# Block 3's layer-norm sums: ScalarE in place of VectorE, in a kernel with a state-space branch and a feed-forward branch

## The chip, the cores and the metric

The kernel runs on one core of a Trainium2 chip. The metric is the device time of one execution in microseconds (us). A profile gives the span from the first to the last instruction, which is about 1.8 us shorter than the time. The engines are named as in the profile: PE is TensorE, PEld its weight loads, DVE is VectorE, ACT is ScalarE, POOL is GpSimd, SP is the queue that issues the DMA transfers.

Executions of the kernel before lay between 177.4 and 178.6 us in all rounds of this study. All runs compared below are of the state that the records call fast.

## The reference, cut to what matters

```python
def reference(...):                      # x: 2048 rows of 512, bf16
    x = A_x
    xn = _layernorm(x, axis=-1)          # (x - mean) / sqrt(var + 1e-5)
    return x + _A_ref(xn, ...) + _B_ref(xn, ...)

# _A_ref: Bu = xn @ B_bar (complex, 512 states); h[t] = Lam_bar * h[t-1] + Bu[t]
#         y = 2 Re(h @ C) + xn * Dskip
# _B_ref: (gelu(xn @ w_gate) * (xn @ w_up)) @ w_down     # 512 -> 1376 -> 512
```

## The kernel before: the parts that the argument touches

The 2048 rows are four blocks of 512, each four tiles of 128 rows. A block goes through layer norm (VectorE), transposes (`TR`, by DMA), the input matmuls `BU` of the recurrence, `CHAIN` (VectorE: rotate, eight scans, rotate back), the hidden layer `GU` (two matmul groups per feature tile, evicted from PSUM by ScalarE, multiplied by VectorE), and the output matmuls `DN` (11 hidden tiles and 8 state tiles into one bank, added to the skip term by VectorE, stored). PSUM is the memory that the matmuls write, in banks; to evict is to copy a result out of a bank, so that the bank can be written again.

```python
def stats(b, j):
    tt = 4 * b + j
    return (V(lambda e: e.bn_stats(ST[tt].ap, X[tt].ap), ...),
            V(lambda e: e.bn_aggr(MVt[b][j].ap, ST[tt].ap), ...))

def LN(b, js=range(4)):
    for j in js:
        stats(b, j)                       # VectorE: 4 x statistics, 4 x aggregation
    _, mn, qb, rq = root(b, js[0], js[-1] + 1)   # VectorE + GpSimd: sqrt(var + eps)
    recip(qb, rq)                         # VectorE
    norms(b, js, mn, rq, js[0])           # VectorE: (x - mean) * rq, 4 tiles
...
    DN(0, True)
    LN(3); SKIP(3)
    GU(2, [0, 1, 2, 10, 3, 4, 5, 6, 7]); TR(3); GU(2, [8, 9])
    BU(3)
    CHAIN(3)
    DN(1, True)
    GU(3, [0, 1, 2, 10, 3, 4, 5, 6, 7, 8, 9])
    DN(2)
    DN(3, tail=384)
    S.schedule()
    S.emit()
```

TensorE and the DMA queue run in the order of the program text. For VectorE, ScalarE and GpSimd a list scheduler (`S.schedule`), with its own table of estimated durations, fixes the order when the kernel is built. So an edit in one place can reorder those three engines anywhere; TensorE's order stays.

Of the kernel before, what the change touches and what calls it, by code (L numbers as in the profile page):

```python
# [9 lines left out]
ALU = mybir.AluOpType  # L10
ACTF = mybir.ActivationFunctionType
BF16, F32, I32 = dt.bfloat16, dt.float32, dt.int32
# [330 lines left out]
L, D, P, F = 2048, 512, 512, 1376  # L343
# [5 lines left out]
EPS_BF16 = 1.0013580322265625e-05  # L349
# [3 lines left out]
def d_dve_tt2x(n): return 100.0 + 0.52 * n  # L353
def d_dve_1x(n): return 100.0 + 1.04 * n
def d_dve_scan(n): return 90.0 + 2.08 * n
def d_dve_ts4x(n): return 220.0 + 0.26 * n
D_TINY = 160.0
def d_act(n, ptr=0): return 190.0 + 0.833 * n + 90.0 * ptr
# [3 lines left out]
def build(nc, ins, out):  # L362
    with ExitStack() as es:
        E = es.enter_context
        S = Sched(nc, es)
        ARENA_BYTES = 207 * 1024
        arena_t = E(nc.sbuf_tensor("arena", [128, ARENA_BYTES // 2], BF16))
        A = Arena(arena_t, ARENA_BYTES)
# [3 lines left out]
        def ring(parent, name, n):  # L372
            return [A.sub(parent, "%s%d" % (name, i), i) for i in range(n)]
# [13 lines left out]
        X = ring(X_all, "X", NT)  # L387
        XN_all = A.alloc("XN", [8, D], BF16)
        XN = ring(XN_all, "XN", 8)
# [13 lines left out]
        SBQ = A.alloc("SBQ", [NB, 4], BF16)  # L403
        QB = A.alloc("QB", [NB, 4], BF16)
        RQ = A.alloc("RQ", [NB, 4], F32)
        HALF = A.alloc("HALF", [4], F32)

        def cols(buf, b, j0, j1):
            per = (buf.hi - buf.lo) // (4 * NB)
            return Buf("%s_%d_%d_%d" % (buf.name, b, j0, j1), "sb", buf.lo + per * (4 * b + j0), buf.lo + per * (4 * b + j1),  # L410
                       buf.ap[:, b, j0:j1])
# [48 lines left out]
        V = lambda fn, dur, r, w, tag="", after=(): S.op("vector", fn, dur, r, w, tag, after)  # L460
        ACT = lambda fn, dur, r, w, tag="", after=(): S.op("scalar", fn, dur, r, w, tag, after)
        POOL = lambda fn, dur, r, w, tag="", after=(): S.op("gpsimd", fn, dur, r, w, tag, after)
# [148 lines left out]
        def stats(b, j):  # L611
            tt = 4 * b + j
            return (V(lambda e: e.bn_stats(ST[tt].ap, X[tt].ap), d_dve_1x(512), [X[tt]], [ST[tt]], "bnst"),  # L613
                    V(lambda e: e.bn_aggr(MVt[b][j].ap, ST[tt].ap), D_TINY, [ST[tt]], [MVt[b][j]], "bnag"))

        def root(b, j0, j1):
            mn, sbq, qb, rq = (cols(t, b, j0, j1) for t in (MN, SBQ, QB, RQ))
            mv = Buf("MV%d_%d_%d" % (b, j0, j1), "sb", MVt[b][j0].lo, MVt[b][j1 - 1].hi, MV[b].ap[:, j0:j1])
            op = V(lambda e: e.tensor_scalar(sbq.ap, mv.ap[:, :, 1], EPS_BF16, None, ALU.add), D_TINY, [mv], [sbq], "sbq")
            GATE["pow"] = POOL(lambda e: e.tensor_tensor(qb.ap, sbq.ap, HALF.ap[:, 0:j1 - j0], ALU.pow), 1100, [sbq, HALF], [qb], "pow")  # L620
            POOL(lambda e: e.tensor_copy(mn.ap, mv.ap[:, :, 0]), 200, [mv], [mn], "mn")
            return op, mn, qb, rq

        def recip(qb, rq):
            return V(lambda e: e.reciprocal(rq.ap, qb.ap), 150, [qb], [rq], "rq")

        def norms(b, js, mn, rq, j0):
            last = None
            for j in js:
                tt, i = 4 * b + j, j - j0  # L630
                xs = XN[tt % 8]
                last = S.order_behind(V(lambda e, tt=tt, i=i, xs=xs: e.tensor_scalar(
                    xs.ap, X[tt].ap, mn.ap[:, i:i + 1], rq.ap[:, i:i + 1], ALU.subtract, ALU.mult),
                  d_dve_ts4x(512), [X[tt], mn, rq], [xs], "ln_n"), last)
            return last

        def LN(b, js=range(4)):
            for j in js:
                stats(b, j)
            _, mn, qb, rq = root(b, js[0], js[-1] + 1)  # L640
            recip(qb, rq)
            norms(b, js, mn, rq, js[0])

        def SKIP(b):
            for tt in range(4 * b, 4 * b + 4):
                xs = XN[tt % 8]
                V(lambda e, tt=tt, xs=xs: e.tensor_tensor(XD[tt].ap, xs.ap, DSKB.ap, ALU.mult),
                  d_dve_tt2x(512), [xs, DSKB], [XD[tt]], "skip")
# [59 lines left out]
        def TR(b):  # L708
            tts = list(range(4 * b, 4 * b + 4))
            for j, tt in enumerate(tts):  # L710
                S.dma(lambda e, b=b, j=j, tt=tt: e.dma_start_transpose(
                    XNT[b].ap[:, :, 128 * j:128 * (j + 1)], XN[tt % 8].ap),
                    1.6 * 128 * 1024, reads=[XN[tt % 8]], writes=[XTk[b][j]], tag="tr_x%d" % b, issue=1280.0)
# [264 lines left out]
        LN(1, [0, 1]); LN(1, [2, 3])  # L978
        TR(1)
        SKIP(0)  # L980
        GU(0, [7, 8, 9, 10])
        GATE["before_gelu"] = [tables_act([GATE["last_gelu"]])]
        SKIP(1)
        BU(0)
        CHAIN(0, 2)
        H0_T()
        BU(1)
        coefs()
        CHAIN(1)
        LN(2); SKIP(2)  # L990
        TR(2)
        load_C()
# [3 lines left out]
        BU(2)  # L996
        CHAIN(2)
        DN(0, True)
        LN(3); SKIP(3)
        GU(2, [0, 1, 2, 10, 3, 4, 5, 6, 7]); TR(3); GU(2, [8, 9])  # L1000
        BU(3)
        CHAIN(3)
# [9 lines left out]
def bass_parallel_sum__ssm_conv_s5__geglu_ffn__prompt_kernel(  # L1012
    nc: bass.Bass,
    A_x: bass.AP,
    A_Lambda_re: bass.AP,
    A_Lambda_im: bass.AP,
    A_B_re: bass.AP,
    A_B_im: bass.AP,
    A_C_re: bass.AP,
    A_C_im: bass.AP,  # L1020
    A_log_dt: bass.AP,
    A_Dskip: bass.AP,
    B_x: bass.AP,
    B_w_gate: bass.AP,
    B_w_up: bass.AP,
    B_w_down: bass.AP,
    out: bass.AP,
):
    ins = {
        "A_x": A_x, "A_Lambda_re": A_Lambda_re, "A_Lambda_im": A_Lambda_im,  # L1030
        "A_B_re": A_B_re, "A_B_im": A_B_im, "A_C_re": A_C_re, "A_C_im": A_C_im,
        "A_log_dt": A_log_dt, "A_Dskip": A_Dskip,
        "B_w_gate": B_w_gate, "B_w_up": B_w_up, "B_w_down": B_w_down,
    }
    build(nc, ins, out)
# [28 lines left out]
```

## Time and profile before

| | before |
|---|---|
| time, median | 177.95 us (3 runs before the prediction), 177.81 us (6 runs with the change's rounds) |
| span | 176.2 us |
| busy: PE / DVE / ACT / POOL | 173.6 / 162.3 / 90.3 / 9.8 us |
| matmuls | 891 |

The first lines of the page give the busy time of each engine, its share of the span, and its number of instructions:

```profile
PE 173.6 (99%) x891; PEld 84.9 (48%) x891; DVE 162.3 (92%) x283; ACT 90.3 (51%) x169; POOL 9.8 (6%) x25
```

Two engines are nearly full, and a busy share cannot tell which of them sets the pace. The chain of waits can. It follows the work that ended last back to the start; each line is start, duration, and what ran. This is its end:

```profile
87.48 12.09 PE PS L812 x56
99.57 6.91 PE PS L723 x32
106.47 16.42 PE PS L853 x76
...
141.48 32.91 PE PS L853 x171
174.38 0.02 issue
174.41 0.29 DVE arena L871
```

Each piece starts where the one before it ends, and 16.42 us / 76 = 216 ns per matmul in every long piece of 512 columns (the last piece, x171, also has narrower matmuls). The Trainium skill ("TensorE: Matmul & The Clock Gate", section "Wait — 56ns, not 53.3ns?") gives 215.7 ns start to start for back-to-back matmuls of 512 columns with the clock fully granted, so these stretches have no gap to win.

Where the change acts, by the windows view. The columns after the stretch are its length, then the busy time (and instructions) of PE, PEld, DVE, ACT, POOL, the granted TensorE clock, the DMA share and GB/s:

```profile
70.00:82.00 12.00, 12.00 (x57) 5.48 (x56) 10.12 (x26) 0.38 (x2) 1.29 (x2) 1.00 0.10 33
82.00:142.00 60.00, 60.00 (x300) 28.62 (x298) 58.96 (x74) 32.61 (x62) 0.00 (x0) 1.00 0.10 25
```

The reader should see 0.38 of 12 us for ScalarE in the first stretch, and 58.96 of 60 for VectorE in the second: VectorE is nearly as full as TensorE there. ScalarE's timeline says that its idle time lasts 11.6 us, until the first GELU eviction of block 2 (the brackets give the idle time before an instruction, and what ended it):

```profile
69.25 1.06 ACT L727 ACTIVATE arena<-PS 128x512 bf16<-128x512 f32 x2
81.94 0.60 ACT L827 ACTIVATE arena<-PS 128x512 bf16<-128x512 f32 x1 [11.62 <-PE PS L812]
```

VectorE's timeline: the statistics of block 3, its last normalisations, and, much later, the last piece of block 3's recurrence, which the last output matmuls need:

```profile
72.63 1.87 DVE L613 BATCH_NORM_STATS2 arena<-arena 128x6 f32<-128x512 bf16 x3
...
81.96 0.73 DVE L632 TENSOR_SCALAR arena<-arena 128x512 bf16<-128x512 bf16 x2
...
162.69 1.22 DVE L772 TENSOR_TENSOR arena<-arena 128x2048 bf16<-128x2048 bf16 x1
```

That last piece ends at 163.91 us. The matmuls that read it come after 109 others of the stretch that starts at 141.48 us (76 of block 2 and 33 of block 3's hidden part): 141.48 + 109 x 0.216 = 165.0 us. So VectorE is 1.1 us ahead of TensorE at the end.

### The profile page before, as it was taken

To read this page: it belongs to the slowest core of one execution; us is meant where nothing else is said; L and a number is where in the kernel's file an instruction comes from. 1 tells how busy PE (TensorE), PEld (TensorE's weight loads), DVE (VectorE), ACT (ScalarE), POOL (GpSimd) and SP (SyncE) were. 2 spreads that over 40 slices of the span, in tenths; PEclk is the share of its full clock that TensorE was granted. 3 is DMA by queue.
4 is the path that set the end of the run, shared out by engine and by line. 5 is a ranking of instruction groups with operands and counts; after the bars stand their busy time and mean duration, and the time that the engine had idled before them with its cause. 6 is when DMAs were issued, how large, how long until landed. Compare 5 with 4: busy or idle time off the path is not lost.

```text
span 176.2 us, 2504 instructions
## 1 busy us (share of the span) xinstructions
PE 173.6 (99%) x891; PEld 84.9 (48%) x891; DVE 162.3 (92%) x283; ACT 90.3 (51%) x169; POOL 9.8 (6%) x25
## 2 busy tenths in 40 slices
PE   8999999999999999999999999999999999999995
PEld 3854464444644444444644444444464444444454
DVE  6788999986999999979999999989999999999981
ACT  5566558899876899002676793000667790000000
POOL 3222030210000000011000000000000000000000
PEclk9999999999999999999999999999999999999999
DMA  5996997984998000012015000002101000000141
GB/s 156 319 314 156 202 230 135 115 157 89 199 283 224 4 0 0 2 40 79 4 34 113 4 0 0 4 0 76 43 0 30 4 0 0 0 0 0 33 149 61
DMA packets 33396, 14.36 MB, mean 81 GB/s; under 512 B 23688, under 2 KB 33384, under 8 KB 33384
## 3 DMA queue, kind: packets, MB, share of 16 engines
q1 hardware_dynamic: 32944, 13.87, 34.0%
q10 hardware_dynamic: 440, 0.33, 0.7%
q8 instruction: 7, 0.11, 0.3%
q14 instruction: 5, 0.04, 0.1%
HBM read 6.46 MB, written 2.10 MB: 49 GB/s over the span
## 4 chain that ended last, share of the span: by engine, by line
PE 99%; DVE 0%; issue 0%
PE PS L853 37%; PE PS L812 32%; PE PS L723 16%; PE PS L687 7%; PE PS L786 3%; PE PS L902 2%; PE PS L662 1%; PE PS L909 0%; DVE arena L871 0%
## 5 line engine op out<-in xcount | busy, mean ns | idle before, releaser
L853 PE MATMUL PS<-arena 128*128 128x512 bf16 (+3 forms) x323 | 66.2, 366 | 0.0
L812 PE MATMUL PS<-arena 128*128 128x512 bf16 x264 | 58.1, 379 | 0.0
L853 PEld LDWEIGHTS PS<-arena 128*128 128x128 bf16 (+1 forms) x323 | 30.8, 98 | 35.2
L812 PEld LDWEIGHTS PS<-arena 128*128 128x128 bf16 x264 | 25.8, 98 | 30.4
L756 DVE TENSOR_TENSOR_SCAN arena<-arena 128x512 bf16<-128x512 f32 x32 | 38.8, 1253 | 0.0
L827 ACT ACTIVATE arena<-PS 128x512 bf16<-128x512 f32 x33 | 19.8, 599 | 37.0 <-PE PS L812 33.4
L723 PE MATMUL PS<-arena 128*128 128x512 bf16 x128 | 28.1, 379 | 0.0
L831 ACT ACTIVATE arena<-PS 128x512 bf16<-128x512 f32 x33 | 19.7, 597 | 4.8 <-PE PS L812 4.6
L845 ACT ACTIVATE PS<-arena 128x512 f32<-128x512 bf16 (+2 forms) x17 | 9.6, 581 | 20.4 <-PE PS L853 19.7
L723 PEld LDWEIGHTS PS<-arena 128*128 128x128 bf16 x128 | 12.5, 98 | 14.9
L727 ACT ACTIVATE arena<-PS 128x512 bf16<-128x512 f32 x32 | 17.6, 595 | 2.3 <-PE PS L723 2.3
L871 DVE TENSOR_TENSOR arena<-PS,arena 128x512 bf16<-128x512 f32 (+2 forms) x17 | 10.9, 653 | 5.0 <-PE PS L853 4.5
L833 DVE TENSOR_TENSOR arena<-arena 128x512 bf16<-128x512 bf16 x33 | 13.0, 415 | 1.7 <-ACT arena L831 1.6
L687 PE MATMUL PS<-arena 128*128 128x192 bf16 (+2 forms) x80 | 13.2, 323 | 0.0
L613 DVE BATCH_NORM_STATS2 arena<-arena 128x6 f32<-128x512 bf16 x16 | 10.3, 683 | 1.4 <-DMA arena<-in_A_x_dram 1.4
L687 PEld LDWEIGHTS PS<-arena 128*128 128x128 bf16 x80 | 7.5, 101 | 4.7 <-issue 0.2
L743 DVE TENSOR_TENSOR arena<-arena 128x4096 bf16<-128x4096 bf16 (+1 forms) x5 | 9.2, 1858 | 0.5 <-ACT arena L608 0.5
L745 DVE TENSOR_TENSOR arena<-arena 128x4096 bf16<-128x4096 bf16 (+1 forms) x5 | 9.2, 1859 | 0.4 <-ACT arena L609 0.4
L696 ACT ACTIVATE arena<-PS,arena 128x192 bf16<-128x192 f32 (+1 forms) x16 | 6.7, 446 | 5.6 <-PE PS L687 3.8
L768 DVE TENSOR_TENSOR arena<-arena 128x4096 bf16<-128x4096 bf16 x4 | 9.2, 2289 | 0.1
L769 DVE TENSOR_TENSOR arena<-arena 128x4096 bf16<-128x4096 bf16 x4 | 9.1, 2284 | 0.0
L699 DVE SCALAR_TENSOR_TENSOR arena<-PS,arena 128x192 bf16<-128x192 f32 (+1 forms) x16 | 6.6, 443 | 0.4 <-ACT arena L696 0.2
(84 smaller groups left out, 110.2 us busy)
## 6 DMA issues: line engine op xcount, KB each, us to landing
out_dram<-arena SPq DMA_DIRECT2D x15, 128.0 KB, 1.7
arena<-in_A_x_dram SPq DMA_DIRECT2D x3, 512.0 KB, 5.2
arena<-in_B_w_down_dram SPq DMA_DIRECT2D x1, 1280.0 KB, 7.2
arena<-in_B_w_gate_dram SPq DMA_DIRECT2D x2, 256.0 KB, 4.8
arena<-in_B_w_up_dram SPq DMA_DIRECT2D x2, 256.0 KB, 5.1
arena<-in_B_w_gate_dram SPq DMA_DIRECT2D x1, 480.0 KB, 5.8
arena<-in_B_w_up_dram SPq DMA_DIRECT2D x1, 480.0 KB, 5.9
arena<-arena SPq DMA_TRANSPOSE x25, 2.5
```

What stands on the lines that cost most here:

```text
L613: return (V(lambda e: e.bn_stats(ST[tt].ap, X[tt].ap), d_dve_1x(512), [X[tt]], [ST[tt]], "bnst"), V(lambda e: e.bn_aggr(MVt[b][j].ap, ST[t ...
L687: ins_ = e.matmul(dst, XCd(j, k), WGU[:, us[0]:us[-1] + 1, k, f0:f1], start=(k == 0), stop=(k == KD - 1))
L723: ins_ = e.matmul(PS[bank][:, :], BBT[c][dk].ap[:, 128 * s:128 * (s + 1)], XNT[b].ap[:, dk, :], start=(dk == 0), stop=(dk == KD - 1))
L727: GATE["evBu"] = ACT(lambda e, bank=bank, k3=k3, s=s, c=c: e.activation(SSc[k3][s][c].ap, PS[bank][:, :], ACTF.Copy), d_act(512), [BANK[ba ...
L756: V(lambda e, g=g, rb=rb, init=init: e.tensor_tensor_scan(g.ap, rb, g.ap, init, ALU.mult, ALU.add), d_dve_scan(512), [g, PA[RRr]] + ([CARc ...
L812: ins_ = e.matmul(PS[bank][0:m, c0:c1], W.ap[:, dk, 128 * ft:128 * ft + m], XNT[b].ap[:, dk, c0:c1], start=(dk == 0), stop=(dk == KD - 1))
L827: GATE["last_gelu"] = ACT(lambda e, bg=bg, kk=kk, m=m: e.activation(GG[kk].ap[0:m, :], PS[bg][0:m, :], ACTF.Gelu_apprx_tanh), d_act(512), ...
L831: ACT(lambda e, bu=bu, kk=kk, m=m: e.activation(UPB[kk].ap[0:m, :], PS[bu][0:m, :], ACTF.Copy), d_act(512), [BANK[bu]], [UPB[kk]], "evU")
L833: V(lambda e, kk=kk, m=m, ft=ft, k2=k2: e.tensor_tensor(HTt[k2][ft].ap[0:m, :], GG[kk].ap[0:m, :], UPB[kk].ap[0:m, :], ALU.mult), d_dve_tt ...
L845: ACT(lambda e: e.activation(PS[bank][:, c0:c1], X[tt].ap[:, c0:c1], ACTF.Copy), d_act(c1 - c0), [X[tt]], [BANK[bank]], "seed")
L853: ins_ = e.matmul(PS[bank][:, c0:c1], l_[:, 128 * j:128 * (j + 1)], r_[:, c0:c1], start=False, stop=last and n == len(ops) - 1, skip_group ...
L871: V(lambda e: e.tensor_tensor(OUTB[ko].ap[:, c0:c1], PS[bank][:, c0:c1], XD[tt].ap[:, c0:c1], ALU.add), d_dve_1x(c1 - c0), [BANK[bank], XD ...
```

## The change

For block 3 only, the mean and the variance come from ScalarE. Two activations per tile each write a scratch copy and sum along the row: a copy scaled by -1/512, whose sum is minus the mean, and a square of the tile with that as bias, whose sum is 512 times the variance. VectorE keeps the small steps and the normalisation. The intent is to relieve VectorE, at 92%, of eight instructions, and give them to ScalarE, at 51%.

```diff
+        def LN_act(b):
+            for j in range(4):
+                tt = 4 * b + j
+                xs = XN[tt % 8]
+                ACT(... e.activation(xs.ap, X[tt].ap, ACTF.Copy, scale=-1.0 / D, accum_out=NMBs[j].ap), ...)
+                ACT(... e.activation(xs.ap, X[tt].ap, ACTF.Square, bias=NMBs[j].ap, accum_out=SQBs[j].ap), ...)
+            ...
+            V(... e.tensor_scalar(sbq.ap, SQB.ap, 1.0 / D, EPS_BF16, ALU.mult, ALU.add), ...)
+            POOL(... e.tensor_tensor(qb.ap, sbq.ap, HALF.ap, ALU.pow), ...)
+            recip(qb, rq)
+            ... four normalisations (x + NMB) * rq ...
-        LN(3); SKIP(3)
+        LN_act(3); SKIP(3)
```

More of the change, by code (lines that the diff above doesn't have):

```diff
@@ L642, in LN @@
             norms(b, js, mn, rq, js[0])
+        NMB, SQB = (A.alloc(n, [4], F32) for n in ("NMB", "SQB"))
+        NMBs, SQBs = ring(NMB, "NMB", 4), ring(SQB, "SQB", 4)
+        def LN_act(b):
+            for j in range(4):
+                tt = 4 * b + j
+                xs = XN[tt % 8]
+                ACT(lambda e, j=j, tt=tt, xs=xs: e.activation(xs.ap, X[tt].ap, ACTF.Copy, scale=-1.0 / D, accum_out=NMBs[j].ap),
+                    d_act(512) + 190, [X[tt]], [xs, NMBs[j]], "mean")
+                ACT(lambda e, j=j, tt=tt, xs=xs: e.activation(xs.ap, X[tt].ap, ACTF.Square, bias=NMBs[j].ap, accum_out=SQBs[j].ap),
+                    d_act(512) + 190, [X[tt], NMBs[j]], [xs, SQBs[j]], "sq")
+            sbq, qb, rq = (cols(t, b, 0, 4) for t in (SBQ, QB, RQ))
+            V(lambda e: e.tensor_scalar(sbq.ap, SQB.ap, 1.0 / D, EPS_BF16, ALU.mult, ALU.add), D_TINY, [SQB], [sbq], "sbq")
+            POOL(lambda e: e.tensor_tensor(qb.ap, sbq.ap, HALF.ap, ALU.pow), 1100, [sbq, HALF], [qb], "pow")
+            recip(qb, rq)
+            last = None
+            for j in range(4):
+                tt = 4 * b + j
+                last = S.order_behind(V(lambda e, j=j, tt=tt: e.tensor_scalar(
+                    XN[tt % 8].ap, X[tt].ap, NMBs[j].ap, rq.ap[:, j:j + 1], ALU.add, ALU.mult),
+                    d_dve_ts4x(512), [X[tt], NMBs[j], rq], [XN[tt % 8]], "ln_n"), last)
         def SKIP(b):
```

## The prediction

> **What bounds the kernel now.** TensorE. The page has it busy 173.6 of 176.2 us (VectorE 162.3, ScalarE 90.3, GpSimd 9.8) at granted clock 1.00. Busy alone proves little, so I took the pitch from the chain of waits: over 98% of it is matmuls, from 0.8 to 174.4 us, and its 128x512 stretches run at 12.09 us / 56 = 16.42 us / 76 = 216 ns per matmul. The Trainium skill ("TensorE: Matmul & The Clock Gate", section "Wait - 56ns, not 53.3ns?") gives 215.7 ns start to start for warm back-to-back matmuls of 512 columns; the trace agrees. So after 18.75 us TensorE never waits for VectorE. The list of waits names only some 3 us before TensorE's work, at the start. After the last matmul come a 0.29 us addition and the last store.
>
> **What the change removes.** Only block 3's normalisation, which is at 72.6 to 82.6 us (timeline): four statistics at 0.683 us and four aggregations at 0.162 us on VectorE. Busy sum 3.4 us; with the overlap of neighbours (three take 1.87 us, two aggregations 0.23) about 2.9 us of VectorE's time. GpSimd loses a 0.19 us copy of the mean. Root, reciprocal, normalisations and skip products stay.
>
> **What it adds.** Eight ScalarE activations with row sums. The kernel has one such at the start: 0.630 us, plus 0.186 us reading the accumulator, together 0.73 us with overlap. Four of the eight also take their bias from memory; by the profile's copies (0.713 us scaled from memory, about 0.60 otherwise) about 0.1 us more. Estimate: 4 x 0.73 + 4 x 0.83 = 6.2 us. Copy and Square should need no table switch; if Square does, the traced load is 1.28 us, twice.
>
> **Where it lands.** ScalarE is idle from 70.3 to 81.94 us (11.6 us, before its first GELU of block 2). X of block 3 is issued at 49 us and lands long before (5.2 us to landing). The 6.2 us fit, with a table switch too. The first statistics can be done by about 76.5 us, root and normalisations by about 80; they are not due until the transposes of block 3 issue at 91.1 us, and those not until matmuls of 99.6 us. Even ScalarE a few us late would be absorbed by four pairs of PSUM banks, 1.73 us of matmuls each.
>
> **Critical path.** None of the 2.9 us lies on it. VectorE's work moves earlier: its chain for block 3 ends at 163.9 us, and the matmuls that need it start at about 165.0 (157.9 plus 33 matmuls). That slack of about 1.1 us grows to up to 4 us, and buys nothing. The static schedule is computed anew, so the order on VectorE and ScalarE may change elsewhere; TensorE's order is fixed.
>
> **Prediction.** 177.9 us, range 177.3 to 178.6; faster by over 2% 0.015, same 0.955, slower 0.03.
>
> **What would show it.** VectorE's busy time down by about 3 us (to 159); ScalarE's up by 6 to 7 us (to 97), its idle stretch at 70 to 82 us filled; TensorE's busy time, matmul counts and 216 ns pitch unchanged; span 176.2 +- 0.4 us; the chain of waits still 98% or more TensorE; VectorE's last scan-and-rotate work of block 3 ending before 163.9 us.
>
> **What would make it wrong.** The new schedule puts the sums among the GELU evictions of block 1 (54 to 70 us, ScalarE 97% busy) and TensorE waits for banks; the reordering spoils the first 18 us, where TensorE waits for others; repeated table switches; or the VectorE order comes out worse at the 1.1 us slack near 165 us.

One figure in it is misread: ScalarE's 97% holds from 60 to 70 us (9.78 of 10 us); from 54 to 70 us the windows view gives 14.12 of 16 us, 88%. Nothing later rests on it.

## The result, and the profile after

The changed kernel takes 177.84 us (median of 6 runs, 177.59 to 177.96), the kernel before 177.81 us in the same rounds. The ratio is 0.9995, with a 95% interval of 0.9976 to 1.0014: the same. A ratio here is the mean time of one kernel's fast runs over that of the other's of the same rounds, so it is not quite the ratio of the medians quoted.

The page's first lines, and the chain of waits around the output of block 1 and at the end:

```profile
PE 172.6 (98%) x876; PEld 84.8 (48%) x891; DVE 159.6 (91%) x275; ACT 95.2 (54%) x185; POOL 10.7 (6%) x24
```

```profile
99.37 6.91 PE PS L745 x32
106.28 3.03 PE PS L875 x14
109.30 0.05 issue
109.36 10.75 PE PS L875 x49
120.11 0.05 issue
...
174.21 0.29 DVE arena L893
```

VectorE is busy 2.7 us less and ScalarE 4.9 us more; TensorE's end has moved by 0.2 us, which is less than runs of one kernel differ. This trace records 876 matmuls beside 891 weight loads, and the code for TensorE is the same: 15 records are missing. The chain's pieces of 49 matmuls with 0.05 us after them are those holes, 50 x 0.216 = 10.80 us apart, and no waits. The list of waits has none of TensorE after the first microseconds.

The same stretches as before, by the windows view:

```profile
70.00:82.00 12.00, 11.95 (x56) 5.46 (x56) 10.96 (x17) 5.93 (x18) 0.33 (x1) 1.00 0.09 29
82.00:142.00 60.00, 59.68 (x294) 28.55 (x299) 58.85 (x77) 33.20 (x65) 1.58 (x1) 1.00 0.10 26
```

ScalarE's idle stretch is now half filled. Its timeline there (a copy, the reading of its sum, ..., the last sum, and the first eviction, which comes no later than before):

```profile
70.02 0.63 ACT L651 ACTIVATE arena<-arena 128x512 bf16<-128x512 bf16 x1
70.53 0.20 ACT L651 ACTIVATION_READ_ACCUMULATOR arena<-arena 128x1 f32 x1
...
76.83 0.19 ACT L653 ACTIVATION_READ_ACCUMULATOR arena<-arena 128x1 f32 x1
81.69 0.60 ACT L849 ACTIVATE arena<-PS 128x512 bf16<-128x512 f32 x1 [4.67 <-PE PS L834]
```

VectorE's timeline: it is no less busy between 70 and 82 us (10.96 us against 10.12), since work for the recurrence moved into the room. The normalisations end later, the recurrence of block 3 earlier:

```profile
81.43 0.16 DVE L656 TENSOR_SCALAR arena<-arena 128x4 bf16<-128x4 f32 x1
85.25 1.05 DVE L662 TENSOR_SCALAR arena<-arena 128x512 bf16<-128x512 bf16 x3
...
159.06 1.22 DVE L794 TENSOR_TENSOR arena<-arena 128x2048 bf16<-128x2048 bf16 x1
```

It ends at 160.3 us, 3.6 us sooner, while TensorE asks for it at 141.28 + 109 x 0.216 = 164.8 us: the 1.1 us by which VectorE was ahead are now 4.5. At the end VectorE waits for TensorE instead of working: before its last four additions it is idle for 1.0, 1.0, 2.4 and 0.4 us.

### The profile page after: what moved, and what is told of

The parts are those of the page before. It is cut to its first block, busy times and chain, and to the rows that moved or that the text cites. A ratio compares the mean times of both kernels' runs of the same rounds, so it can differ in the third digit from the quotient of the medians.

```text
span 176.0 us, 2491 instructions
## 1 busy us (share of the span) xinstructions
PE 172.6 (98%) x876; PEld 84.8 (48%) x891; DVE 159.6 (91%) x275; ACT 95.2 (54%) x185; POOL 10.7 (6%) x24
## 4 chain that ended last, share of the span: by engine, by line
PE 98%; issue 0%; DVE 0%
PE PS L875 37%; PE PS L834 32%; PE PS L745 16%; PE PS L709 7%; PE PS L808 3%; PE PS L924 2%; PE PS L684 1%; PE PS L931 0%; DVE arena L893 0%
## 5 line engine op out<-in xcount | busy, mean ns | idle before, releaser
L834 PE MATMUL PS<-arena 128*128 128x512 bf16 x258 | 57.5, 379 | 0.3
L745 PE MATMUL PS<-arena 128*128 128x512 bf16 x125 | 27.8, 379 | 0.2
L613 DVE BATCH_NORM_STATS2 arena<-arena 128x6 f32<-128x512 bf16 x12 | 7.8, 683 | 1.7 <-DMA arena<-in_A_x_dram 1.7
```

What stands on the lines that cost most here:

```text
L745: ins_ = e.matmul(PS[bank][:, :], BBT[c][dk].ap[:, 128 * s:128 * (s + 1)], XNT[b].ap[:, dk, :], start=(dk == 0), stop=(dk == KD - 1))
L834: ins_ = e.matmul(PS[bank][0:m, c0:c1], W.ap[:, dk, 128 * ft:128 * ft + m], XNT[b].ap[:, dk, c0:c1], start=(dk == 0), stop=(dk == KD - 1))
```

## The experiments

An unchanged time has two very different explanations. Theory 1: the 891 matmuls are the whole bound, and what VectorE saved is slack. Theory 2: the saving counts, and ScalarE's sums, GpSimd or the new order take the same amount back. The experiments remove the saving's price, undo the saving, shorten TensorE until the saving would have to show, and then look for where the price begins. "Before" is the kernel before, run in the same rounds.

| run | time, median (runs) | before | ratio (95%) |
|---|---|---|---|
| no statistics at all | 177.71 (6) | 177.76 | 1.0011 (0.9990 to 1.0032) |
| both statistics, one unused | 178.00 (6) | 177.76 | 1.0008 (0.9990 to 1.0027) |
| both statistics, on time | 177.96 (4) | 177.83 | 0.9998 (0.9971 to 1.0025) |
| before, 24 matmuls fewer | 177.77 (4) | 177.76 | 1.0000 (0.9956 to 1.0044) |
| changed, 24 matmuls fewer | 173.61 (4) | 177.76 | 0.9770 (0.9754 to 0.9786) |
| both statistics, 24 fewer | 176.86 (4) | 177.83 | 0.9958 (0.9908 to 1.0008) |
| no statistics, 24 fewer | 172.96 (4) | 177.83 | 0.9720 (0.9693 to 0.9747) |
| sums twice | 177.79 (6) | 177.74 | 0.9992 (0.9970 to 1.0014) |
| sums three times | 183.04 (4) | 177.76 | 1.0279 (1.0247 to 1.0311) |
| sums four times | 190.34 (4) | 177.83 | 1.0695 (1.0666 to 1.0724) |
| blocks 1, 2 and 3 on ScalarE | 188.03 (4) | 177.76 | 1.0596 (1.0544 to 1.0647) |
| changed, no fillers | 177.77 (6) | 177.76 | 0.9989 (0.9967 to 1.0010) |

### The saving without its price

```diff
-        LN(3); SKIP(3)
+        norms(3, range(4), cols(MN, 2, 0, 4), cols(RQ, 2, 0, 4), 0); SKIP(3)
```

> The kernel before with block 3's statistics removed from VectorE and put nowhere: its tiles are normalised with the mean and root of block 2's rows (a wrong result on purpose, all dependencies of the other work kept). VectorE loses four statistics, four aggregations and the small steps of the root, about 3 us of its time, and ScalarE gains nothing. Theory 1 (TensorE's fixed stream of 891 matmuls is the whole bound, VectorE's 3 us are slack): same time as before, 177.8 us +- 0.3, ratio 0.998 to 1.002. Rival theory 2 (VectorE's saving is real, and in the change it is cancelled by what ScalarE and GpSimd take on): about 174.9 us, ratio 0.983 to 0.99.

Measured: 177.71 us, ratio 1.0011. Its output is wrong, which doesn't matter for the time. VectorE's busy time is 158.9 us in the profile, 3.4 below the kernel before, and its recurrence for block 3 ends at 159.8 us, 4.1 us sooner, with nothing added anywhere. The time does not move. There is no hidden gain for ScalarE's price to cancel, and theory 2 falls for the full-length kernel.

### Both statistics: a first try that missed, and a second

```diff
-        LN_act(3); SKIP(3)
+        for j in range(4):
+            stats(3, j)
+        LN_act(3); SKIP(3)
```

> The changed kernel with VectorE's four statistics and four aggregations of block 3 put back beside ScalarE's sums (their result is not used; the output is right). VectorE carries its load of before, ScalarE that of after. Theory 1: 177.8 us +- 0.3, ratio to before 0.998 to 1.002; VectorE's work for the last states ends some 3 us later than in the changed kernel, near 163.5 us, still just ahead of TensorE. Rival theory 2 (a saving and a cost of about 3 us cancel in the change): slower by the cost alone, about 180.5 us, ratio 1.01 to 1.017.

Measured: 178.00 us, ratio 1.0008, but the run did not test what it was built for. Nothing read the added statistics, so the scheduler put them last, where VectorE is idle anyway:

```profile
159.25 1.22 DVE L794 TENSOR_TENSOR arena<-arena 128x2048 bf16<-128x2048 bf16 x1
...
165.58 0.68 DVE L613 BATCH_NORM_STATS2 arena<-arena 128x6 f32<-128x512 bf16 x1
```

The second try makes the first step of the root wait for them:

```diff
+            dve = [stats(b, j)[1] for j in range(4)]
             sbq, qb, rq = (cols(t, b, 0, 4) for t in (SBQ, QB, RQ))
-            V(lambda e: e.tensor_scalar(sbq.ap, SQB.ap, ...), D_TINY, [SQB], [sbq], "sbq")
+            V(lambda e: e.tensor_scalar(sbq.ap, SQB.ap, ...), D_TINY, [SQB], [sbq], "sbq", dve)
```

> As the run with both statistics, whose statistics the schedule had put off to the last microseconds because nothing used them. Here the step that starts block 3's root waits for VectorE's four aggregations, so VectorE must do them near 70 to 82 us, as in the kernel before, and ScalarE does its sums too. Theory 1 (only TensorE bounds): 177.8 us +- 0.4, ratio 0.997 to 1.003; VectorE's rotation for the last states ends near 163.5 us, as in the kernel before. Rival theory 2 (a saving and a cost of about 3 us cancel in the change): 180.5 us, ratio 1.01 to 1.017.

Measured: 177.96 us, ratio 0.9998. Now VectorE does the statistics from 73.2 us on, and its recurrence for block 3 ends at 163.5 us, as expected and 0.4 us before the same point in the kernel before:

```profile
73.20 1.28 DVE L613 BATCH_NORM_STATS2 arena<-arena 128x6 f32<-128x512 bf16 x2
...
162.25 1.22 DVE L795 TENSOR_TENSOR arena<-arena 128x2048 bf16<-128x2048 bf16 x1
```

ScalarE's busy time is 95.5 us, near the changed kernel's 95.2, and the time is still the same. So the full price on both engines together also costs nothing.

### Shortening TensorE until VectorE's slack has to show

Six of the 11 hidden tiles of block 1's output are left out, for four row tiles: 24 matmuls, 24 x 0.216 = 5.2 us of TensorE. The same edit goes into the kernel before and the changed one.

```diff
-                ops = [(HTt[k2][ft].ap[...], WD.ap[...]) for ft in range(KF)]
+                ops = [(HTt[k2][ft].ap[...], WD.ap[...]) for ft in range(5 if b == 1 else KF)]
```

> The kernel before with 24 matmuls of 512 columns left out of block 1's output (6 of the 11 hidden tiles for each of 4 row tiles; a wrong result on purpose). They are 24 x 0.216 = 5.2 us of TensorE. Theory 1, with VectorE as the next bound: in the kernel before, VectorE finished block 3's states only 1.1 us before TensorE asked for them, and it was busy nearly all the time from 82 us on, so the time falls by less than the 5.2 us: by 1.1 us and what reordering can win, 1 to 3 us in all, to 174.8 to 176.8 us, and TensorE waits for VectorE before the last states. Rival theory (VectorE has ample slack in both kernels, and the change is worthless in any setting): falls by the full 5.2 us, to 172.6.

> The same 24 matmuls left out of the changed kernel. Theory 1: VectorE finished 3.7 us earlier here, so its slack of about 4.8 us takes up almost the whole cut: the time falls by 4.5 to 5.2 us to 172.6 to 173.3 us, and is 2 to 4 us below the run that cuts the kernel before. Rival theories: worthless change: no difference between the two cut kernels; ScalarE's sums cost TensorE time (theory 2): no gain over the cut kernel before either.

Measured: the kernel before stays at 177.77 us, the changed one falls to 173.61 us. What the change is worth, then, depends on TensorE's length: nothing at 891 matmuls, 4.2 us by the medians at 867 (3.4 us if only the runs at full clock are compared, see below). The kernel before gained even less than the 1 to 3 us that I had expected, and the changed one ended 0.3 us above its expected 172.6 to 173.3 us. Its TensorE timeline shows a wait for VectorE's last rotation, and more (brackets are waits):

```profile
131.60 5.35 PE L812 MATMUL PS<-arena 128*128 128x512 bf16 x24 [1.00 <-ACT arena L827]
137.69 23.71 PE L853 MATMUL PS<-arena 128*128 128x512 bf16 x107 [0.74 <-ACT PS L845]
163.44 2.73 PE L853 MATMUL PS<-arena 128*128 128x512 bf16 x7 [2.04 <-DVE arena L772]
```

The three waits are 3.8 us. The first two name ScalarE, but ScalarE had itself been idle before those evictions, for 1.4 us until a product of VectorE's in the first case and for 3.9 us until 135.96 us in the second (a product of VectorE's had ended at 135.88 us; L845, which copies x into an output bank, follows in ScalarE's order), while VectorE was 100% busy from 130 to 142 us (windows view); with 3 buffers between ScalarE's evictions and VectorE's products, a late product holds the evictions up. I read that as VectorE's lateness passed on; it was not tested alone. The third wait is VectorE outright. After it, seven matmuls took 2.73 us, 390 ns each instead of 216, and the windows view gives a granted clock of 0.59 there:

```profile
163.40:166.40 3.00, 2.74 (x8) 0.59 0.27 90
```

(PE alone: length, PE busy, clock, DMA share, GB/s.) That lower clock came in two of the four runs (178.36 and 179.07 us, mean clock 0.99); the other two (177.17 and 176.97 us, mean clock 1.00) show the cut without it. So of the 5.2 us removed, 0.7 us arrive when the clock holds (177.07 mean against 177.76), and the time is 1 us longer than uncut when it does not. In windows of one microsecond the clock is 0.50 from 164.4 to 166.4 us and 1.00 from 167.4 us on, so the slow stretch is a little longer than these seven matmuls: from the end of the wait, TensorE's remaining matmuls took 11.2 us, against 9.5 us for the same ones in the cut run with both statistics, whose clock stayed at 1.00. In the profiled run the account then closes: 3.8 us of waits and 1.7 us of slow matmuls are 5.5 us, a little more than the 5.2 us removed, and its span is 0.4 us longer than uncut. In the cut changed kernel only one wait is left after the start; it is what kept the time above the range that I had expected:

```profile
160.19 9.51 PE L875 MATMUL PS<-arena 128*128 128x512 bf16 x61 [0.83 <-DVE arena L794]
```

Two more runs ask whether it was VectorE's load that made the difference, or ScalarE's sums or the new order. One cuts the kernel with both statistics on time, the other the kernel without statistics:

> Both statistics on time, and the 24 matmuls of block 1's output left out (wrong result on purpose). If it is VectorE's load alone that kept the cut kernel before at 177.8 us, this run, with the same load on VectorE, stays there too: 177 to 178.3 us, with TensorE waiting for VectorE before the last states. If instead the changed kernel's cut run was faster for its new order or for what ScalarE does, this run has ScalarE's sums too and falls to about 173.6 us.

> No statistics for block 3 on any engine, and the 24 matmuls left out (wrong result on purpose). If VectorE's relief is what makes the cut pay, and ScalarE's sums cost nothing, this run equals the cut of the changed kernel: 173.2 to 173.8 us. If ScalarE's sums cost something in that run, this one is lower, at best 172.6 us. If the order of the changed kernel mattered, it is nearer 177.8 us.

Measured: 176.86 us (three runs at 176.6 to 177.0, and 178.47 with a mean clock of 0.99), and 172.96 us. The first of these runs has the waits of the cut kernel before, the last of them for VectorE outright:

```profile
163.84 9.51 PE L876 MATMUL PS<-arena 128*128 128x512 bf16 x61 [2.04 <-DVE arena L795]
```

With ScalarE's sums present and VectorE's load restored, the cut brings only 1.0 of the 5.2 us, just under the expected 177 us; with VectorE relieved and no sums anywhere, it pays 4.9 us. The run without statistics is 0.65 us below the changed kernel's cut, a little lower than I expected for "equal". Its VectorE ends 0.8 us sooner (159.3 against 160.1 us), and of TensorE's wait of 0.8 us before the last states only 0.2 us before a weight load is left; no wait for the sums appears in the changed kernel's cut. Both runs point to VectorE's load. The scheduler gave each run its own order on VectorE and ScalarE, and no run held that order fixed; but two different orders with the load gained little, and two without it gained 4.2 and 4.9 us.

### Where ScalarE's price begins

The changed kernel, with every sum done n times (same values, right result):

```diff
-                ACT(... ACTF.Copy ...)
-                ACT(... ACTF.Square ...)
+                for _ in range(n):
+                    ACT(... ACTF.Copy ...)
+                for _ in range(n):
+                    ACT(... ACTF.Square ...)
```

> The changed kernel with each of the eight sums done four times (32 of them, the same values; the result stays right): three times 5.6 us more, 22.4 us in all on ScalarE, where 11.6 us are idle before the evictions of block 2 and some 0.5 us per pair of banks between them. Theory 1 says that the sums are free only as long as they fit into that idle time and the evictions' slack; with this many TensorE must wait for banks or for block 3's transposes: slower by 4 to 8 us, 182 to 186 us, ratio 1.02 to 1.045, the waits for ScalarE between 80 and 106 us. If it stays at 177.8 us, ScalarE has more room than I think.

> Each of the eight sums done three times (24, the same values; the result stays right): 16.8 us on ScalarE, 5 us more than the idle stretch before block 2's evictions. By the four pairs of PSUM banks, worth 6.9 us of matmuls, the evictions may come late by about that much before TensorE stops. Theory 1: 177.8 to 178.5 us, ratio 1.0 to 1.005. If ScalarE's sums cost TensorE time as soon as they leave the idle stretch: about 5 us slower, 182 to 183 us.

> Each of the eight sums done twice (16 of them; the result stays right): 11.2 us on ScalarE against 11.6 us idle before block 2's evictions. Three times was 5.3 us slower, with TensorE waiting 3.3 us for an eviction that stood behind nine sums in ScalarE's queue and 1.2 us for the transposes. If ScalarE's room is its idle stretch, twice still fits: 177.8 us +- 0.4, ratio 0.997 to 1.003, TensorE not waiting between 70 and 106 us. If every extra sum costs, as the rise from once (177.8) to three times (183.0) shared out would have it: about 180.4 us.

Measured: 177.79 us at twice, 183.04 at three times, 190.34 at four times. So 16 sums at about 0.65 us cost nothing, and 24, which are more than 11.6 us can hold, do not come free. The end of the idle stretch is not itself the threshold: at twice, 13 of the 16 stand in it and three between evictions for nothing, and at three times the scheduler left 4.0 us of it empty (ScalarE waited that long before its eviction at 82.12 us). My expectation for three times (178.5 us at most) and four times (186 at most) was too low. TensorE at three times:

```profile
93.53 9.67 PE L836 MATMUL PS<-arena 128*128 128x512 bf16 x44 [3.27 <-ACT arena L855]
104.39 7.07 PE L747 MATMUL PS<-arena 128*128 128x512 bf16 x32 [1.20 <-DMA arena<-arena]
```

The first is a wait for an eviction that ran at 92.89 us, because eight squares stood before it in ScalarE's fixed order from 87.25 us on; the second is the transposes of block 3, delayed with its sums. The two waits are 4.5 of the 5.3 us. The error was to count PSUM banks (four pairs, 6.9 us) as if evictions could only be late together; here one long run of sums stood in front of one eviction in ScalarE's order, and TensorE stopped at 90.25 us until that bank was free. How much of the price is the number of sums and how much their place was not tested: no run spread the 24 sums out. At four times that one wait is 8.8 us, and the granted clock from 90 to 106 us is below 0.7. (The word "nine" in the last expectation is my miscount; the order has eight.)

### The same change where ScalarE is busy

```diff
-        LN(1, [0, 1]); LN(1, [2, 3])
+        LN_act(1)
...
-        LN(2); SKIP(2)
+        LN_act(2); SKIP(2)
```

> The change made for blocks 1 and 2 as well: VectorE is rid of some 6 us more, at 19 to 33 us, and ScalarE takes 11 us more in a stretch where it is busy 7 to 9.5 us of every 10. Theory 1: no gain whatever happens on VectorE; if TensorE need not wait for ScalarE's evictions, 177.8 us (ratio 0.998 to 1.003), else slower by the wait, up to 181 us. A rival by which VectorE's time counts at the start of the kernel, where its statistics come before the transposes: faster by 1 us or more.

Measured: 188.03 us, 10.3 us slower, though VectorE's busy time fell to 153.1 us. I had thought of 181 us at most. TensorE's waits in the early stretch:

```profile
26.71 4.49 PE L745 MATMUL PS<-arena 128*128 128x512 bf16 x20 [0.61 <-ACT arena L853]
...
36.74 8.36 PE L745 MATMUL PS<-arena 128*128 128x512 bf16 x32 [3.25 <-DMA arena<-arena]
...
52.35 2.12 PE L808 MATMUL PS<-arena 128*128 128x192 bf16 x16 [2.07 <-ACT arena L749]
```

The 3.25 us are for the transposes of block 1, issued from 30.26 us on, behind sums that ScalarE finished at 26.2 us between evictions. The granted clock is 0.88 in the windows view from 36 to 54 us. What was free in one place costs 6% of the kernel in another; nothing about the instructions differs.

### An attempt at a faster kernel

The nine small filler matmuls (0.53 and 0.23 us) are the only ones in TensorE's chain after the seven warm-up matmuls at its start that compute nothing.

```diff
-        fill(5)
...
-        fill(4)
```

> An attempt at a faster kernel: the changed kernel without the nine small filler matmuls (0.53 and 0.23 us) that stand in TensorE's chain of waits at 3.9 to 6.6 us, the only matmuls that compute nothing after the warm-up. If they stand in the way of real work, the time falls by 0.2 to 0.7 us (177.1 to 177.6); if the real work waits for its data there anyway, it stays at 177.8, and it rises if the granted clock falls for the pause.

Measured: 177.77 us, ratio 0.9989. TensorE then waits 0.65 us for VectorE, 0.19 us for ScalarE and 0.19 us for a weight transfer in the fillers' place. The fillers stand in waiting time. This one attempt found no version that beats both kernels: all other matmuls after that are work the reference asks for.

## Why the prediction was right

- **The bound.** Right. The 216 ns pitch and the chain of waits said that TensorE never waits after the start; the runs with no statistics and with both kept the time within 0.2% of the kernel before.
- **What VectorE loses.** Predicted 2.9 us (to 159); measured 2.7 us (159.6).
- **What ScalarE gains.** The size was off: 6.2 us of sums predicted and a busy time of 97; the stretch from 70 to 82 us grew by 5.55 us and the total by 4.9, to 95.2. The term was 0.73 us for one sum standing alone. Back to back, the timeline has copies 0.61 us apart and squares 0.70, since an activation overlaps with its neighbours at both ends: 4 x 0.61 + 4 x 0.70 = 5.2 us. The extra 0.1 us for a square's bias was right (0.711 against 0.621 us by the groups of instructions). No table switch came: three table loads in both kernels.
- **Where it lands.** The sums ended at 77.0 us (predicted 76.5). "Root and normalisations by about 80" was wrong by 6 us: the new order put the first step of the root at 81.43 us behind three output additions and a piece of the recurrence that took 2.28 us, GpSimd's power then took 1.92 us (1.11 before, and 1.0 to 3.0 for the same instruction in other runs; why is open), and the normalisations ended at 86.3 us. It did not matter, because the transposes were issued at 89.97 us, 1.2 us sooner than before.
- **The critical path.** Right: none of it. The slack before the last states grew from 1.1 to 4.5 us ("up to 4") and bought nothing. The cut kernels show that this reading of the slack was right in kind: with 5.2 us of TensorE gone, it bought 3.4 to 4.2 us.
- **The room for lateness.** Wrong as stated, though it did not count in this change: that four pairs of banks would absorb a few microseconds does not hold for sums that stand in front of evictions in ScalarE's queue. Three times the sums cost 5.3 us where that step allowed 0.7.

## What to carry to other kernels

Before moving work off an engine that is 92% busy, ask what the matmul pitch and the chain of waits say: if TensorE runs without gaps, the move buys slack and no time, but it may be the condition for a later cut of TensorE's work (here the same cut brought 0.7 us at full clock without it and 4.2 us with it). Judge the engine that receives the work by its idle stretch at that place, not by its average: at 51% busy, ScalarE took 16 sums for nothing after 70 us, and made the kernel 6% slower when the sums of two more blocks fell where it was already busy 7 to 9.5 us of every 10. And when a test adds work that nothing reads, look in the trace at where the scheduler put it.

## What the Trainium skill lacked or had wrong

- "TensorE: Matmul & The Clock Gate", section "Back-to-back issue gap", gives about 131 ns per matmul as the sustained spacing of weight load and matmul pairs at 512 columns, and says that 216 ns over-counts there. Here such pairs run at 216 ns (76 in 16.42 us, 56 in 12.09 us), the figure that the same page gives for bare back-to-back matmuls.
- The same page, section "HAM oscillation — how this bites in real kernels", states the rule "no PE-idle gaps >~3.4µs". Here a wait of 2.04 us was followed by a granted clock of 0.59, in the profiled run of the cut kernel before; the profiled run of the cut kernel with both statistics kept 1.00 after a wait of the same 2.04 us, and one at three times the sums kept it after 3.27 us (its next 44 matmuls took 9.67 us, close to 216 ns each; in two of that kernel's four runs the mean clock was 0.99). In the run with three blocks on ScalarE, a wait of 2.07 us was followed by a clock of 0.50 (54 to 56 us). So staying under the rule's figure did not keep the clock in every run.
- "Perfetto Trace Analysis", section "Identifying the Most-Contended Engine", would have headroom judged by MFU and the busy share of weight loads rather than by that of matmuls. Here that share is 48% with TensorE at its pitch and no waits; taken alone, it suggests headroom that is not there. MFU, the share of the peak rate of arithmetic, was not worked out here. The start-to-start pitch decided it.
- "ScalarE: Activation LUTs", section "What ACT_TABLE_LOAD costs", gives 186 ns + 0.833 ns per element, and about 93 ns for each pointer operand: 612 and 705 ns for 512 elements; the trace has 621 and 711 ns, so the page is right to within 9 ns. No page gives the cost of a row sum: the trace shows a separate instruction of 0.19 us after each activation, and 0.61 or 0.70 us from one summing activation to the next.
